# Output projections and side scores of the last layer, held back eight tiles instead of three and none

## The chip, the cores and the metric

The kernel runs on 1 core of one Trainium2 chip. The metric is the device time of one execution in microseconds (us). The time given is the median of three runs; the profile is of one further execution.

## The reference

Four layers follow each other, x = x + attention(layernorm(x)), over a sequence of 2048 rows of width 640 with 32 heads of 20 columns. Layers 0 and 2 attend in a causal window of 256 keys, layers 1 and 3 to all 2048 keys. The change is in layer 3, which computes:

```
def _B_ref(x, wqkv, wo):
    qkv = (x @ wqkv).reshape(B, S, 3, H, Dh).transpose(2, 0, 3, 1, 4)
    q, k, v = qkv[0], qkv[1], qkv[2]
    p = softmax(einsum("bhqd,bhkd->bhqk", q, k) * Dh ** -0.5)
    o = einsum("bhqk,bhkd->bhqd", p, v)
    return o.transpose(0, 2, 1, 3).reshape(B, S, D) @ wo
...
x = x + _B_ref(_layernorm(x), B_wqkv, B_wo)
```

## The kernel before

**Units and tiles.** The queries are cut into 4 chunks of 512 rows (c = 0 to 3), the heads into 8 groups of four (g = 0 to 7). A unit is one (layer, chunk, group). Its scores are made in banks: one block of 128 keys against 512 queries for one head fills one PSUM bank. A full unit has 16 key blocks x 4 heads = 64 banks. The main loop advances in tiles of three banks (rarely two or four): TensorE (PE) makes the scores of a tile (L1316), ScalarE (ACT) takes their exponential (L1347), and PE multiplies the exponentials of some tiles ago with the values (L1380). Tiles alternate between PSUM banks 0 to 2 and 3 to 5. Bank 7 collects a unit's output; bank 6 is left in the late stage for everything else.

**Side scores.** In layer 3, for c > 0 but for unit (3, 1, 0), six of the 64 banks of a unit (four in the very last unit) do not go through ACT. The generator `t_side` makes their scores one bank at a time in bank 6 (L912) and lets VectorE (DVE) compute the exponential by arithmetic (L918 to L946). It takes the units in order and works ahead of the main loop as far as the unit's keys and queries are loaded and one of five result buffers is free. Before, it waits only until the unit's loads have been issued (`loaded`) and the late stage has begun. At a unit's last bank, `side_need` forces whatever side scores are missing, and `side_done` forces their exponentials before the unit's last value products (L1389).

**Loads.** `load_ahead` issues the loads of the next unit (values L778, queries L790, keys L792, on SP's queue) when one of three buffers is free, which is when an earlier unit's last scores and values products have been issued.

**Normalise, pack, project.** When a unit ends, `finish_unit` casts its output from bank 7 into the tile `on` (L864). After every second unit `push_tail` starts `t_tail` for the pair: sums of the exponentials, reciprocal, spreading and scaling (L1090), in steps with waits of two tiles between them. Last comes `settle`: for the chunks 1 to 3 of layer 3, the scaled rows of four heads, which stand 32 partitions apart, are packed to dense rows of 128 by small transfers inside SBUF (L1103, SP's queue, nine for a pair). For the last two groups of chunk 3 nothing is packed. After the group that completes a chunk (g = 7), and after group 5 of chunk 3, `settle` waits three tiles (L1108) and then pushes the next task: `t_out`, the output projection of the chunk (matmuls by L300, added to x at L568, stored to HBM at L574), or `t_before_last`, the partial projection of the first six groups of chunk 3 (L591, L599). `t_out` makes eight pieces of 128 rows x 320 columns; with dense rows a piece is five row blocks of four matmuls.

**What sets the order.** All instructions are put out by one program, tile by tile, and each engine takes its own in that order. `state["tick"]` counts tiles. After each tile's exponential, `pump` runs tasks: first the tails that are awake, then the tasks of `todo` by due time, as far as a credit (0.45 a tile in this stage) reaches. `("wait", n)` puts a task to sleep until the tick has advanced by n. A task that uses bank 6 takes it by `take_m` and gives it back by `drop_m`. `keep_clock` fills tiles in which PE has little to do with matmuls that nobody reads (L300 masks,ident). Loops that force work (`require`, `side_need`, `side_done`) advance the tick without a tile when nothing is awake. `next_tile` makes a tile of four banks only when no tail exists and all tasks sleep.

Of the kernel before, what the change touches and what calls it, by code (L numbers as in the profile page):

```python
# [48 lines left out]
def kernel(  # L49
# [78 lines left out]
    def packed(l, c):  # L128

        return l == 3 and c > 0  # L130
# [56 lines left out]
    state = {"tick": 0, "held": None, "credit": 0.0, "early": True, "act": True, "unit": 0, "heat": 0.0, "carry": 0.0, "least": 0.0, "floor": 0.0, "owed": 0}  # L187
# [16 lines left out]
    def push(name, gen, need, left):  # L204
        lead = 0
        if type(name) is tuple and need <= first_use(1, NC - 1, 0):

            chain = {"out": True, "ln": name[1] == 1, "v": name[1] == 1 and name[-1] == 0}
            lead = 5 * chain.get(name[0], False)
            if name[0] in ("k", "q"):  # L210
                lead = 7 if name[1] == 1 and name[-1] == 0 else 2

            if name[0] == "stats" or name[:2] == ("ln", 0):
                lead = 5
        insort(todo, Task(name, gen, need, left, lead))
# [68 lines left out]
    def require(what):  # L284
        n = 0
        while what not in ready:
            n += 1
            assert n < 100000, what
            t = choose(False, state["unit"] if n < 400 else 1 << 30)
            if t is None:  # L290
                state["tick"] += 1
                continue
            state["credit"] = max(state["credit"] - advance(t), -1.0)
# [465 lines left out]
    def load_unit(u):  # L759

        l, c, g = u.l, u.c, u.g
        key = (l, c, g)
        if u.windowed:
            live["qa"] += 1
            live["ka"] += 1
            ka[c, g], qa[c, g] = ka_free.popleft(), qa_free.popleft()
            for j in range(4):
                rows = slice((4 * g + j) * DH, (4 * g + j + 1) * DH)
                strip = slice(32 * j, 32 * j + DH)
                nc.sync.dma_start(out=qa[c, g][strip, :], in_=q_d[l][c, rows, :])  # L770
                nc.sync.dma_start(
                    out=ka[c, g][strip, :], in_=k_d[l][rows, c * C : (c + 1) * C]
                )
            return
        k0, k1 = key_blocks(l, u.part)
        live["vt"] += 1
        vt[key] = kvp.tile([P, NT * 4 * VW], BF16, name="vt", tag="vt")
        nc.sync.dma_start(  # L778
            out=vt[key][:, k0 * 4 * VW : k1 * 4 * VW],
            in_=v_d[l][:, g, k0 * 4 * VW : k1 * 4 * VW],  # L780
        )
        live["kt"] += 1
        live["qt"] += 1
        kt[key] = kts[loads[0] % 3]
        qt[key] = qts[loads[0] % 4]
        loads[0] += 1
        for j in range(4):
            rows = slice((4 * g + j) * DH, (4 * g + j + 1) * DH)
            strip = slice(32 * j, 32 * j + DH)
            nc.sync.dma_start(out=qt[key][strip, :], in_=q_d[l][c, rows, :])  # L790
            cols = slice(k0 * P, k1 * P)
            nc.sync.dma_start(out=kt[key][strip, cols], in_=k_d[l][rows, cols])  # L792

    def unit_needs(u):
        l, c, g = u.l, u.c, u.g
        if (l, c) == (0, 0):
            return [("qk", l, c, g)]
        k0, k1 = key_blocks(l, u.part)
        chunks = range(k0 // 4, k1 // 4)
        blocks = range(80 * g // P, (80 * g + 79) // P + 1)  # L800
        if u.windowed:
            return [(n, l, c, b) for b in blocks for n in "qk"]
        return ["kts"] + [("q", l, c, b) for b in blocks] + [
            n
            for cc in chunks
            for n in [("k", l, cc, b) for b in blocks] + [("v", l, cc, g // 4)]
        ]

    loaded = set()

    def ensure_loaded(u, force):
        if id(u) in loaded:
            return
        needs = unit_needs(u)
        if force:
            for n in needs:
                require(n)
        elif any(n not in ready for n in needs) or any(
            live[t] >= cap[t] for t in (("ka", "qa") if u.windowed else ("kt", "vt", "qt"))
        ):  # L820
            return
        load_unit(u)
        loaded.add(id(u))

    def start_unit(u):
        for n in unit_needs(u):
# [47 lines left out]
    side = {"credit": 0.0, "gen": None, "tiles": None, "late": False}  # L874
# [22 lines left out]
    def t_side():  # L897

        V = nc.vector
        while aside:  # L900
            u = aside[0]
            for pair in range(len(u.aside) // 2):
                while id(u) not in loaded or (u.l == 3 and not side["late"]):
                    yield None
                for i in range(2):
                    yield "bank"
                    xi, xm, xw = side["tiles"]
                    if u.l == 3:
                        mseq[0] += 1
                        mfree[6] = (state["tick"] + 2, mseq[0])  # L910
                        kc, j = u.aside[2 * pair + i]
                        nc.tensor.matmul(  # L912
                            ps[:, 6, :], lhsT=u.k(kc, j), rhs=u.q(j, 0, 4), start=True, stop=True
                        )
                        side["psum"] = ps[:, 6, :]
                    scored = side.setdefault("scored", {})
                    scored[id(u)] = scored.get(id(u), 0) + 1
                    V.tensor_scalar(  # L918
                        out=xi.bitcast(I32)[:, i * C : (i + 1) * C], in0=side["psum"],
                        scalar1=SCALE * LOG2E * FIX, scalar2=-127.0 * FIX, op0=ALU.mult, op1=ALU.max,  # L920
                    )
                    yield 0.7
                V.tensor_scalar(
                    out=xm, in0=xi.bitcast(U16)[:, 0::2],
                    scalar1=E1 / FIX, scalar2=E0, op0=ALU.mult, op1=ALU.add,
                )
                yield 0.7
                power = xw.bitcast(I16)[:, 0 : 2 * C]
                V.tensor_scalar(
                    out=power, in0=xi.bitcast(I16)[:, 1::2],  # L930
                    scalar1=127.0, scalar2=128.0, op0=ALU.add, op1=ALU.mult,
                )
                yield 0.7
                V.scalar_tensor_tensor(
                    out=xi, in0=xm, scalar=EA, in1=xm, op0=ALU.add, op1=ALU.mult
                )
                yield 1.2
                while not side["out"]:
                    yield None
                pt = side["out"].popleft()  # L940
                po = pt.rearrange("p a b -> p (a b)")
                V.scalar_tensor_tensor(
                    out=po, in0=xi, scalar=EB, in1=xm, op0=ALU.add, op1=ALU.mult
                )
                yield 1.2
                V.tensor_tensor(out=po, in0=po, in1=power.bitcast(BF16), op=ALU.mult)  # L946
                side_out.setdefault(id(u), []).append(pt)
                yield 0.7
            aside.popleft()
# [145 lines left out]
    def settle(l, c, g, oT):  # L1095
        on = ons[l, c]
        if packed(l, c) and not ((l, c) == (3, NC - 1) and g >= G - 2):
            for j in range(4):
                r, a = (4 * g + j) * DH, 0
                while a < DH:  # L1100
                    b, o = divmod(r + a, P)
                    n = min(DH - a, P - o)
                    nc.sync.dma_start(  # L1103
                        out=on[o : o + n, b, :], in_=oT[32 * j + a : 32 * j + a + n, :]
                    )
                    a += n
            if g == G - 1 or (l, c, g) == (3, NC - 1, G - 3):
                yield ("wait", 3)  # L1108
        ready.add(("tail", l, c, g))
        if (l, c, g) == (3, NC - 1, G - 3):  # L1110
            push("before_last", t_before_last(), 0, 8.0)
        if g == G - 1:
            while any(("tail", l, c, n) not in ready for n in range(G)):
                yield ("wait", 1)
            need = first_use(l + 1, c, 0) if l < 3 else len(units) + c
            push(("out", l, c), t_out(l, c), need, 9.0)
            if l < 3:
                push_layer(l + 1, c)
# [82 lines left out]
    with tc.manual_schedule():  # L1201
# [17 lines left out]
        while n < last_layer:  # L1219
            size = 2 if len(tiles) % 2 and narrow(banks[n][0]) else 3  # L1220
            u = banks[n][0]
# [57 lines left out]
        while ended is None or t < ended + 8:  # L1279
# [3 lines left out]
            if t < len(tiles) or banks:  # L1283
# [9 lines left out]
                for b in cur:  # L1293
                    u = b[0]
# [69 lines left out]
            for n in range(2 if n_b == 0 or t > closed + 1 else 0):  # L1364
                u = pts[0][3][0] if pts else None
# [111 lines left out]
```

## Time and profile before

| | us |
|---|---|
| median of three runs (2224.45 to 2225.8) | 2225.43 |
| the profiled execution | 2229.77 |
| its span, first to last instruction | 2228.1 |
| busy: PE, DVE, ACT, POOL | 1933.2, 1200.5, 2141.2, 484.0 |
| mean granted clock of TensorE | 0.989 of full speed |

The last layer takes about the last 650 us of the span. In the profile's lines a group of instructions is given by its line, its engine, the operation and the tiles that it writes and reads; PEld is PE's loading of weights, SPq the queue on which SP issues transfers. "idle before" is the time in which the engine had nothing to do ahead of an instruction, with what released it. L300 is the line of a helper: the output projections, the sums and the fillers of the clock all carry it, and are told apart by their tiles (wop,on; sel,on; masks,ident).

### The profile page before, as it was taken

Reading aid. Unit: us, or ns where it says so; the run is one execution under the profiler, and the core shown is the slowest. Engines: PE = TensorE matmul, PEld = TensorE weight load, DVE = VectorE, ACT = ScalarE, POOL = GpSimd, SP = SyncE. Lnnn points to the kernel's source line nnn. Section 1 sums busy time; section 2 is a strip of 40 time slices with the busy share of each in tenths; the row PEclk is TensorE's granted clock in tenths of the full one; section 3 lists DMA queues with packets and bytes.
Section 4 is the critical chain, followed back from the end, with each engine's and each line's share of the span. In section 5 each row is a group of like instructions: output and inputs, shape, how many; then the busy total and the mean of one; then the engine's idle time right before and its main releaser. Section 6 shows DMA issues by size and latency. Waiting matters only on the chain.

```text
span 2228.1 us, 70079 instructions
## 1 busy us (share of the span) xinstructions
PE 1933.2 (87%) x30410; PEld 757.7 (34%) x30411; DVE 1200.5 (54%) x2190; ACT 2141.2 (96%) x1734; POOL 484.0 (22%) x950
## 2 busy tenths in 40 slices
PE   8889998988888888888888888888888888888888
PEld 4444443333333333333333433333322222222222
DVE  6656564434445455444554533532577767776774
ACT  7899899999999999999999999999999999999998
POOL 6664545200230114301143113511000000000000
PEclk9999999999999999999999999999999999999999
DMA  6233223321211223112230123122211111111100
GB/s 199 74 99 90 83 83 94 99 78 46 76 39 35 67 60 99 34 39 65 63 99 23 52 71 103 28 67 57 60 55 32 31 35 40 32 31 38 44 25 16
DMA packets 88404, 137.09 MB, mean 62 GB/s; under 512 B 20766, under 2 KB 63486, under 8 KB 88094
## 3 DMA queue, kind: packets, MB, share of 16 engines
q1 hardware_dynamic: 68878, 79.43, 12.8%
q0 software_dynamic: 19216, 53.17, 8.1%
q8 instruction: 238, 3.90, 0.7%
q14 instruction: 72, 0.59, 0.1%
HBM read 99.52 MB, written 27.79 MB: 57 GB/s over the span
## 4 chain that ended last, share of the span: by engine, by line
ACT 51%; PE 22%; issue 17%; DVE 7%; DMA 1%; POOL 1%; SPq 0%; ACTq 0%; DVEq 0%; POOLq 0%
ACT pt L1347 50%; PE ps L300 13%; PE ps L1316 6%; PE ps L1380 2%; DVE on L1090 1%; DVE st L323 1%; DVE pt L1429 1%; DMA wqk<-in_B_wqkv_dram 1%; PE ps L1086 1%; PE ps L437 0%; DVE x_sb L568 0%; DVE on L864 0%; SPq L1103 0%; DVE raw_o L918 0%; DVE xnT L323 0%
## 5 line engine op out<-in xcount | busy, mean ns | idle before, releaser
L1347 ACT ACTIVATE pt<-ps 128x1536 bf16<-128x1536 f32 (+2 forms) x1656 | 2104.2, 1456 | 55.4 <-PE ps L1316 45.7
L1316 PE MATMUL ps<-qt,kt 32*128 32x512 bf16 x3960 | 547.3, 386 | 91.1 <-ACT pt L1347 82.0
L300 PE MATMUL ps<-masks,ident 128*32 128x512 bf16 x5840 | 513.8, 389 | 118.3 <-ACT pt L1347 68.4
L1380 PE MATMUL ps<-pt,vt 128*21 128x512 bf16 x3904 | 400.0, 385 | 1.5 <-issue 1.0
L1316 PEld LDWEIGHTS <-kt 32*128 32x128 bf16 x3960 | 163.4, 91 | 551.4 <-issue 536.0
L300 PEld LDWEIGHTS <-ident 128*32 128x32 bf16 x5840 | 165.3, 94 | 351.8 <-issue 339.7
L1419 POOL TENSOR_SCALAR_AFFINE_SELECT pt<-pt 128x256 bf16<-128x256 bf16 (+2 forms) x505 | 214.8, 447 | 189.7 <-ACT pt L1347 187.0
L300 PE MATMUL ps<-xnT,wqk 128*32 128x512 bf16 x3320 | 225.3, 384 | 15.2 <-DVE st L323 4.0
L323 DVE CAST st<-ps 128x512 bf16<-128x512 f32 x134 | 92.7, 692 | 234.8 <-PE ps L300 228.3
L300 PE MATMUL ps<-wop,on 128*32 128x320 bf16 x3712 | 161.6, 303 | 11.9 <-DMA on<-on 5.0
L918 DVE TENSOR_SCALAR xnT<-ps 128x512 int32<-128x512 f32 x136 | 93.5, 688 | 134.2 <-PE ps L912 123.3
L1429 DVE TENSOR_TENSOR pt<-pt,masks 128x512 bf16<-128x512 bf16 (+4 forms) x267 | 112.9, 438 | 96.7 <-ACT pt L1347 94.5
L1380 PEld LDWEIGHTS <-vt 128*21 128x21 bf16 x3912 | 105.1, 91 | 125.0 <-issue 92.9
L568 DVE TENSOR_TENSOR x_sb<-x_sb,ps 128x320 bf16<-128x320 bf16 x120 | 58.3, 486 | 155.5 <-PE ps L300 155.2
L300 PEld LDWEIGHTS <-on 128*32 128x32 bf16 x5760 | 113.7, 95 | 80.9 <-issue 57.7
L1316 PE MATMUL ps<-qa,ka 32*128 32x384 bf16 (+2 forms) x1408 | 114.9, 275 | 27.5 <-ACT pt L1347 24.5
L300 PE MATMUL ps<-wv,xnT 128*32 128x320 bf16 x2560 | 115.2, 301 | 8.3 <-DVE on L1090 2.2
L1090 DVE TENSOR_TENSOR on<-on,ps 128x512 bf16<-128x512 bf16 x128 | 86.3, 683 | 58.3 <-PE ps L1086 56.1
L300 PEld LDWEIGHTS <-wqk 128*32 128x32 bf16 x3320 | 77.3, 96 | 114.6 <-issue 62.4
L864 DVE CAST on<-ps 128x512 bf16<-128x512 f32 x112 | 76.9, 687 | 66.2 <-PE ps L1389 41.9
L536 POOL DMA_DIRECT2D k_d<-st x75 | 43.0, 574 | 236.8 <-DVE st L323 226.9
L404 POOL TENSOR_SCALAR rstd<-mv 128x4 f32<-128x4 f32 x15 | 3.7, 249 | 381.6 <-DVE mv L391 373.4
(100 smaller groups left out, 1544.1 us busy)
## 6 DMA issues: line engine op xcount, KB each, us to landing
vt<-v_d SPq DMA_DIRECT2D x48, 336.0 KB
kt<-k_d SPq DMA_DIRECT2D x192, 80.0 KB
wqk<-in_B_wqkv_dram POOLq DMA_DIRECT2D x80, 160.0 KB, 3.4
wqk<-in_A_wqkv_dram POOLq DMA_DIRECT2D x70, 160.0 KB, 3.5
k_d<-st POOLq DMA_DIRECT2D x75, 128.0 KB, 2.6
q_d<-st POOLq DMA_DIRECT2D x75, 128.0 KB, 2.2
qt<-q_d SPq DMA_DIRECT2D x384, 20.0 KB
v_d<-vs POOLq DMA_DIRECT2D x16, 336.0 KB, 3.2
```

Of the source, the lines that this page charges most:

```text
L300: nc.tensor.matmul(out_[r], lhsT=lhsT[:, r], rhs=rhs, start=start, stop=stop)
L323: nc.vector.tensor_copy(out=out_, in_=in_)
L536: nc.gpsimd.dma_start(out=dst, in_=staging.pop())
L568: nc.vector.tensor_tensor(out=xv, in0=had, in1=yp, op=ALU.add)
L864: nc.vector.tensor_copy(out=oT, in_=op)
L918: V.tensor_scalar(out=xi.bitcast(I32)[:, i * C : (i + 1) * C], in0=side["psum"], scalar1=SCALE * LOG2E * FIX, scalar2=-127.0 * FIX, op0=AL ...
L1090: nc.vector.tensor_tensor(out=oT, in0=oT, in1=zb, op=ALU.mult)
L1316: nc.tensor.matmul(sp[:, i, col * P : (col + qn) * P], lhsT=u.k(kc, j), rhs=u.q(j, q0, qn), start=True, stop=True,)
L1347: nc.scalar.activation(out=pt[:, i:k, b0 * P :], in_=sp[:, i:k, b0 * P :], func=ACT.Exp, scale=SCALE,)
L1380: nc.tensor.matmul(op[32 * j : 32 * j + VW, q0 * P : (q0 + qn) * P], lhsT=u.v(kc, j), rhs=pg[:, i, col * P : (col + qn) * P], start=(first ...
L1419: nc.gpsimd.affine_select(out=v, in_=v, compare_op=ALU.is_gt if later else ALU.is_ge, fill=0.0, base=0, pattern=[[0, k - i], [-1 if later ...
L1429: nc.vector.tensor_tensor(out=pt_[:, i:k, cols], in0=pt_[:, i:k, cols], in1=mv_, op=ALU.mult)
```

## The change

The wait between packing and projecting grows from three tiles to eight. `loaded`, a set before, keeps the tick at which a unit's loads were issued, and the side scores of a unit of layer 3 start only eight ticks after it.

```diff
-    loaded = set()
+    loaded = {}
...
         load_unit(u)
-        loaded.add(id(u))
+        loaded[id(u)] = state["tick"]
...
             for pair in range(len(u.aside) // 2):
-                while id(u) not in loaded or (u.l == 3 and not side["late"]):
+                while id(u) not in loaded or (
+                    u.l == 3 and (not side["late"] or state["tick"] < loaded[id(u)] + 8)
+                ):
                     yield None
...
             if g == G - 1 or (l, c, g) == (3, NC - 1, G - 3):
-                yield ("wait", 3)
+                yield ("wait", 8)
         ready.add(("tail", l, c, g))
```

## The prediction

> **What bounds the kernel now.** I read the page's busy times first, then its costliest groups, then the view of waits after 1500 us (the last layer), and then the timeline and the stage table at the two places that the waits led to.
>
> ```profile
> PE 1933.2 (87%) x30410; PEld 757.7 (34%) x30411; DVE 1200.5 (54%) x2190; ACT 2141.2 (96%) x1734; POOL 484.0 (22%) x950
> ...
> L1347 ACT ACTIVATE pt<-ps 128x1536 bf16<-128x1536 f32 (+2 forms) x1656 | 2104.2, 1456 | 55.4 <-PE ps L1316 45.7
> ...
> L300 PE MATMUL ps<-wop,on 128*32 128x320 bf16 x3712 | 161.6, 303 | 11.9 <-DMA on<-on 5.0
> ```
>
> ACT is busy 96% of the span, with the exponentials of L1347. So an edit shortens the kernel only where it takes away ACT's idle time. The third line names the one operation that the change addresses: output projections that waited 5.0 us for the packing transfers. The waits after 1500 us, first PE's and then all of ACT's:
>
> ```profile
> PE ps L300 <- DMA on<-on: 5.0, 2, 2.5
> ...
> ACT pt L1347 <- PE ps L1316: 11.3, 13, 3.0
> ```
>
> The 5.0 us are two waits of 2.5 us. ACT lacks 11.3 us in the whole of the last layer, so that is nearly all there is to win. Asked by stretch, 5.4 of it lies between 1800 and 1900 us and 5.6 between 2000 and 2100, where the two waits are. The timeline at the first (start, length; idle before in brackets):
>
> ```profile
> 1819.72 6.83 SPq L1103 DMA_DIRECT2D on<-on  x9
> ...
> 1824.62 0.73 PE L300 MATMUL ps<-wop,on 128*32 128x320 bf16 x16
> 1827.87 0.32 PE L300 MATMUL ps<-wop,on 128*32 128x320 bf16 x4 [2.52 <-DMA on<-on]
> ```
>
> ```profile
> 1812.82 13.57 ACT L1347 ACTIVATE pt<-ps 128x1536 bf16<-128x1536 f32 x10
> 1828.83 2.82 ACT L1347 ACTIVATE pt<-ps 128x1536 bf16<-128x1536 f32 x2 [2.44 <-PE ps L1316]
> 1832.50 2.96 ACT L1347 ACTIVATE pt<-ps 128x1536 bf16<-128x1536 f32 x2 [0.85 <-PE ps L1316]
> 1835.93 2.96 ACT L1347 ACTIVATE pt<-ps 128x1536 bf16<-128x1536 f32 x2 [0.47 <-PE ps L1316]
> 1839.87 11.15 ACT L1347 ACTIVATE pt<-ps 128x1536 bf16<-128x1536 f32 x8 [0.97 <-PE ps L1316]
> ```
>
> SP is still issuing the nine packing transfers, 0.71 us apart, when PE starts the projection. Sixteen matmuls (four row blocks) pass, and the fifth block waits for the last transfer. PE takes its matmuls in order, so the next tile's scores stand behind it and ACT runs dry for 2.44 us. Then come three more gaps, with no transfer in sight. The stage table shows why (stretch, busy time of PE, PEld, DVE, ACT and POOL, then granted clock, DMA share, GB/s):
>
> ```profile
> 1825.00:1828.00 3.00, 0.48 (x16) 0.16 (x12) 0.32 (x1) 1.39 (x2) 0.00 (x0) 1.00 0.11 24
> ...
> 1830.00:1832.00 2.00, 1.79 (x15) 0.23 (x11) 1.54 (x3) 1.65 (x2) 0.00 (x0) 0.50 0.23 82
> ...
> 1838.00:1840.00 2.00, 2.00 (x27) 0.62 (x23) 1.15 (x2) 1.03 (x2) 0.00 (x0) 0.52 0.00 0
> 1840.00:1842.00 2.00, 1.94 (x36) 0.57 (x28) 1.76 (x4) 2.00 (x2) 0.00 (x0) 1.00 0.00 0
> ```
>
> Just after the wait the granted clock halves for some 10 us; PE is then full and late for every tile. The second place (2.52 us from 2039.3) has the same pair, 0.50 from about 2041.3 to 2051.5. In 1575 to 1825, 1856 to 2038 and 2070 to 2228 us the table gives 1.00.
>
> **The price of one stall.** Before the first place ACT did ten tiles in 13.57 us, 1.357 each. Its stream stops at 1812.82 + 13.57 = 1826.39 and is whole again at 1839.87. In these 13.48 us it did 6 tiles, worth 8.14, so 5.34 us are lost: 2.44 to the wait, 2.90 to the slow clock. At the second place ACT stops at 2040.37 and is whole at 2052.19 after 5 tiles. At the 6.84 / 5 = 1.368 us of the row before they are worth 6.84 of 11.82, so 4.98 us are lost: 3.02 to the wait, 1.96 to the clock. Together 10.3 us: 5.5 wait, 4.9 clock.
>
> **The longer wait, part by part.** It adds and removes no instruction and no DMA; it starts the projections of chunks 1 and 2, and the partial one of chunk 3, five tiles later. Five tiles are 5 x 1.357 = 6.8 us. The first projection then starts at 1824.6 + 6.8 = 1831.4 and its fifth block about 0.6 later, at 1832.0; the data were there at 1827.87. The margin is 4.1 us; at the second place 2038.6 + 6.8 + 0.6 = 2046.0 against 2041.85, again 4.1. Both stalls go, and with them, I take it, the clock drops: -10.3 us.
>
> What is late next: each pass is eight projections of 20 matmuls (0.86 us each), about 30 us long, so a later start moves its second half further past the end of a unit and into the next pair's normalisation, with which it shares PSUM bank 6 and DVE. Before already shows such meetings: 0.45 us of ACT idle at 1851.47, 0.94 at 2066.97 (the next projection waited 1.62 us for L568, behind L942 of 1.22 and L946 of 0.68), 0.4 near 1600. The bounds of what the shift does to these: at best all 1.8 us go too; at worst each of the two passes gets two more like the dearest, 4 x 0.94 = 3.8 us. I take +0.5, near the rows that exist, because the number of meetings hardly changes; only their place does.
>
> Chunk 3's partial projection (L591) waits only 0.2 us for its data. Moved by 6.8 us, it runs from 2198 to 2207.7 + 6.8 = 2214.5 at most. The last unit's output is cast at 2217.94, so it still ends before the final chain needs it; 3.4 us remain. Cover gone, each of its eight parts left over costs 0.72 us of PE. The one four-bank tile there (2.11 us at 2211.97) needs idle queues and may become three-bank tiles: 4 banks in the 1.76 us to the next tile against 4/3 x 1.357 = 1.81, so nothing.
>
> Meanwhile the tail stays in the queue five tiles longer. Nothing queues behind it: tails come once in two units (52 us from the packing issues at 1767.51 to those at 1819.72). On PE the five tiles are filled with the fillers of the clock (L300 masks,ident), as all tiles without a projection are. SP is not moved past anything: the transfers are issued where they were, and only the four output stores of each pass come later.
>
> **The side scores' wait.** No side score (L912) waits for a load in the trace; PE's waits there are on DVE alone (2.0 and 0.9 us). So nothing is to be gained. What it can delay: the first side score stands at 1578.16, its unit's loads at 1568.88 to 1572.7, six or seven tiles before, so it moves by one or two tiles. Its unit's sixth score (1597.19) is needed only when that unit ends, near 1631, so 34 us cover it. The other units' loads are far ahead: those of the last unit go out at 2141.68, its four side scores follow from 2168.30 on, 26 us or some 19 tiles later; the second unit's are loaded at 1577.14 and scored from 1603.38. I take 0; the ends are -0.9 and +0.9, the size of one meeting on DVE.
>
> **Sum.** -10.3 + 0.5 + 0 = -9.8 us. The profiled execution took 2229.77 us (span 2228.1, 1.7 around it), so it would come to about 2220.0. The median of the shown runs is 2225.43, 4.3 lower; the same -9.8 gives 2215.6 us, -0.44%.
>
> **A rule that speaks against half of this.** The row first: a PE gap of 2.52 us is followed by clock 0.50 twice. The Trainium skill, TensorE: Matmul & The Clock Gate, section "HAM oscillation — how this bites in real kernels", gives as the abstract rule that PE gaps should stay under about 3.4 us. By it a 2.5 us gap is harmless, the drop has another cause and stays, and the sum is -5.5 + 0.5: 2220.4. By the rows the drop belongs to the gap; I go with the rows, since the clock is whole elsewhere in this layer.
>
> **The rivals.**
> 1. The clock drops anyway (its cause is the load mix of the projection pass, not the gap). For it: near 898, 1168 and 1277 us the table shows drops too, where PE only missed 0.85 us here and 1.5 there. Against it: the pass near 1600 has 1.00 throughout. Then only the waits go: 2225.4 - 5.5 + 0.5 = 2220.4. Chance 0.10.
> 2. The later pass collides with the next pair's normalisation and the side scores hard enough to halve the clock by itself, as near 1168 after gaps of 0.85 and 0.43 us. Each place pays 2 to 3 us of clock and two meetings of 0.94: 2 x (2.5 + 1.9) = 8.8 given back, 2215.1 + 8.8 = 2223.9. Against it: the second half of the pass already runs there at 1.00. Chance 0.11.
> 3. The wait doesn't do what it says: it counts the scheduler's ticks, and forced loops advance ticks without a tile. From the first issue to the last landing it takes 1827.87 - 1819.72 = 8.15 us, six tiles; if fewer than two of the five added ticks are real tiles, a shorter stall stays. Then 2224 to 2225.5. For it: only that such loops exist. Chance 0.05.
> 4. Slower: the held-back side scores come due at a unit's end. There the scheduler forces what is missing, and PE and ACT wait for DVE: one pair is 2 x 0.69 + 0.69 + 0.69 + 1.22 + 1.22 + 0.68 = 5.9 us. It decides from two such forced pairs on (11.8 against 9.8); from three on it shows, 17.7 - 9.8 = +7.9, 2233.3. Against it: the load leads of 19 tiles and more, and 34 us of slack at the first unit. Chance 0.05.
>
> **How the numbers follow.** The forecast holds 0.69, and lies by itself between 2213 (the meetings gone too, -1.8) and 2219 (3.8 of them new). For 8 in 10, rival 1 goes in, and the nearer half of rival 2: 2212.8 to 2222.5. About 0.2% (4.45 us) is what a measurement of this kernel tells from no change, so faster means under 2221.0: the forecast with 0.68, rival 1 with 0.08, rival 2 with 0.01, in all 0.77. Within 0.2%: rivals 1 (0.02), 2 (0.10) and 3 (0.05) and 0.01 of the forecast, 0.18. Slower by 0.2%: rival 4 alone, 0.05.
>
> **What would show it.** Right: no "DMA on<-on" among PE's waits; ACT idle after 1500 us down from 11.3 to about 1 to 3 us; granted clock 1.00 from 1575 us on; first projection matmuls of chunks 1 and 2 about 12 us after the first packing issue instead of 4.9 (1819.72 to 1824.62); the last L591 before the last L864. Wrong: clock 0.50 near 1835 or 2045 without a DMA wait (rival 1 or 2); ACT gaps at unit ends with PE behind L942 or L946 (rival 4); an L591 after the last unit.

## The result, and the profile after

The changed kernel takes 2215.88 us (median of 17 runs, 2210.82 to 2227.0) against 2228.07 us (17 runs, 2223.6 to 2235.04) for the kernel before on the same chips. The ratio is 0.9948 with a 95% interval of 0.9937 to 0.996, so between 8.9 and 14.0 us of 2228 are gone. Forecast were 9.8.

The page of the changed kernel (lines moved by two from L923 on, so L1347 is now L1349):

```profile
PE 1919.8 (87%) x30415; PEld 756.1 (34%) x30415; DVE 1199.8 (54%) x2190; ACT 2139.9 (97%) x1734; POOL 482.5 (22%) x950
...
L1349 ACT ACTIVATE pt<-ps 128x1536 bf16<-128x1536 f32 (+2 forms) x1657 | 2104.3, 1456 | 41.8 <-PE ps L1318 32.1
...
L300 PE MATMUL ps<-wop,on 128*32 128x320 bf16 x3712 | 159.8, 301 | 7.1 <-DVE x_sb L568 4.0
```

ACT does the same work (2139.9 us, 2141.2 before) in a shorter span; its idle time ahead of the exponentials went from 55.4 to 41.8 us. The projections no longer wait for "DMA on<-on"; what they wait for most is now their own earlier pieces on DVE, 4.0 us in the whole execution (3.3 before). The first place, in the timeline of the changed kernel:

```profile
1814.41 6.82 SPq L1105 DMA_DIRECT2D on<-on  x9
...
1827.04 0.86 PE L300 MATMUL ps<-wop,on 128*32 128x320 bf16 x20
...
1828.50 0.86 PE L300 MATMUL ps<-wop,on 128*32 128x320 bf16 x20
```

The first piece starts 12.6 us after the first packing issue instead of 4.9 and runs through all its twenty matmuls. ACT's timeline there and at the second place:

```profile
1798.92 40.88 ACT L1349 ACTIVATE pt<-ps 128x1536 bf16<-128x1536 f32 x30
...
2004.48 46.21 ACT L1349 ACTIVATE pt<-ps 128x1536 bf16<-128x1536 f32 x34
2051.63 49.91 ACT L1349 ACTIVATE pt<-ps 128x1536 bf16<-128x1536 f32 x37 [0.94 <-PE ps L1318]
```

Thirty and 34 exponentials in a row, where before the row broke after every one or two. The gap of 0.94 us at the second place was there before too. All of ACT's waits in the last layer, then the stage table at the first place (busy times, then granted clock):

```profile
ACT pt L1349 <- PE ps L1318: 2.4, 6, 0.9
```

```profile
1826.00:1830.00 4.00, 3.67 (x65) 1.66 (x65) 3.96 (x7) 4.00 (x4) 0.00 (x0) 1.00 0.00 0
1830.00:1845.00 15.00, 12.94 (x193) 4.03 (x192) 11.89 (x18) 14.47 (x12) 0.00 (x0) 1.00 0.24 74
```

**A yardstick that leaves the rest out.** The two profiled executions differ by 15.4 us of span, more than the medians, because the clock also dropped at other places in the layers before, and differently in each execution. Both kernels issue the same instructions up to the one four-bank exponential that writes ka near 1570 us. It stands, before and after, here:

```profile
1575.33 2.21 ACT L1347 ACTIVATE ka<-ps 128x2048 bf16<-128x2048 f32 x1
```

```profile
1569.81 2.21 ACT L1349 ACTIVATE ka<-ps 128x2048 bf16<-128x2048 f32 x1
```

So 5.5 us of the difference were there before the change could act. From this point to the end of the span it is 2228.1 - 1575.33 = 652.8 us before and 2212.7 - 1569.81 = 642.9 after: 9.9 us less. The experiments are compared by this stretch.

### The profile page after: what moved, and what is told of

Same layout as the page of the kernel before. It is cut to its first block, busy times and chain, and to the rows that moved or that the text cites. A ratio compares the mean times of both kernels' runs of the same rounds, so it can differ in the third digit from the quotient of the medians.

```text
span 2212.7 us, 70085 instructions
## 1 busy us (share of the span) xinstructions
PE 1919.8 (87%) x30415; PEld 756.1 (34%) x30415; DVE 1199.8 (54%) x2190; ACT 2139.9 (97%) x1734; POOL 482.5 (22%) x950
## 4 chain that ended last, share of the span: by engine, by line
ACT 52%; PE 21%; issue 18%; DVE 6%; DMA 1%; POOL 1%; ACTq 0%; DVEq 0%; POOLq 0%
ACT pt L1349 51%; PE ps L300 12%; PE ps L1318 5%; PE ps L1382 2%; DVE on L1092 1%; DVE st L323 1%; DVE pt L1431 1%; DMA wqk<-in_B_wqkv_dram 1%; PE ps L1088 1%; PE ps L437 0%; DVE on L864 0%; DVE x_sb L568 0%; DVE raw_o L920 0%; POOL pt L1421 0%; DVE xnT L323 0%
## 5 line engine op out<-in xcount | busy, mean ns | idle before, releaser
L1349 ACT ACTIVATE pt<-ps 128x1536 bf16<-128x1536 f32 (+2 forms) x1657 | 2104.3, 1456 | 41.8 <-PE ps L1318 32.1
L568 DVE TENSOR_TENSOR x_sb<-x_sb,ps 128x320 bf16<-128x320 bf16 x120 | 58.3, 486 | 146.8 <-PE ps L300 146.6
L536 POOL DMA_DIRECT2D k_d<-st x75 | 43.0, 573 | 233.2 <-DVE st L323 223.2
```

What stands on the lines that cost most here:

```text
L536: nc.gpsimd.dma_start(out=dst, in_=staging.pop())
L568: nc.vector.tensor_tensor(out=xv, in0=had, in1=yp, op=ALU.add)
L1349: nc.scalar.activation(out=pt[:, i:k, b0 * P :], in_=sp[:, i:k, b0 * P :], func=ACT.Exp, scale=SCALE,)
```

## The experiments

| run | stretch, us | ACT idle in it | PE's wait on on<-on | half clock at the two places | ratio to before (95%) |
|---|---|---|---|---|---|
| before | 652.8 | 11.3 | 5.0 | both, 10.2 and 10.2 us | |
| after | 642.9 | 2.4 | none | none | 0.9948 (0.9937-0.996) |
| after, again | 642.0 | 1.6 | none | none | 0.996 (0.9946-0.9973) |
| longer wait alone | 643.4 | 1.9 | none | none | 0.9957 (0.9946-0.9968) |
| side wait alone | 652.4 | 11.1 | 5.6 | both, 10.2 and 6.8 us | 1.0001 (0.9992-1.0011) |
| early, no rows of the last transfers | 641.9 | 1.9 | none | none | 0.9963 (0.9951-0.9976) |
| four tiles | 649.2 | 8.8 | 5.2 | second only, 6.8 us | 1.0001 (0.9988-1.0015) |
| six tiles | 647.8 | 7.4 | 4.9 | first only, 6.8 us | 0.9986 (0.9972-1.0) |
| 24 tiles | 646.9 | 1.1 | none | none | 0.9977 (0.9965-0.9989) |
| side wait of 48 | 775.1 | 130.0 | none | many | one run, 2350.2 us |
| packing on POOL's queue | 645.7 | 4.5 | none | none | 0.994 (0.9919-0.9961) |
| gap filled | 649.8 | 9.3 | 1.7 | none | 0.9983 (0.9974-0.9992) |
| 24 tiles, chunk 3 eight | 641.2 | 0.7 | none | none | 0.9949 (0.9937-0.9961) |

In the early run and in the one on POOL's queue the partial projection of chunk 3 still waits 0.2 to 0.6 us for its transfers, as before; the column leaves that out. The column on the clock counts the drops right behind the two waits; single drops of 3.4 us elsewhere are named below.

**The two parts apart.** Longer wait alone, in the kernel before:

```diff
-                yield ("wait", 3)
+                yield ("wait", 8)
```

> The longer wait alone; the side scores start as before. The yardstick is the stretch from the four-bank tile (the one exponential that writes ka near 1570 us, which both kernels issue at the same place and ahead of anything changed) to the end of the span: 652.8 us before (2228.1 - 1575.33), 642.9 after (2212.7 - 1569.81). My theory (the whole gain is the longer wait): 642 to 644 us, no wait on on<-on, ACT idle after 1500 us between 1 and 3 us, clock 1.00 at both passes. Rival (the side scores' wait brings part of it): 645 us or more.

Measured: 643.4 us and ratio 0.9957. The other part alone, in the changed kernel:

```diff
-                yield ("wait", 8)
+                yield ("wait", 3)
```

> The side scores' wait alone, with three tiles before the projections. My theory: as before, 651 to 654 us from the four-bank tile to the end, two waits of about 2.5 us on on<-on and two clock drops. Rival (the side scores' wait brings part of it): 650 us or less.

Measured: 652.4 us and ratio 1.0001, with waits of 2.9 and 2.7 us on the transfers. So the longer wait is the whole gain, and the side scores' wait neither gains nor costs anything that these runs can tell (its interval is 0.9992 to 1.0011). The changed kernel run once more beside others:

> The changed kernel as it is, beside the other two on the same chip: 642 to 644.5 us from the four-bank tile to the end, and a ratio to the kernel before between 0.993 and 0.996.

It gave 642.0 us and 0.996, both as expected.

**Is it the gap?** The pass left where it was, without its need of the last rows:

```diff
-                        yp, on[:, g, qb * P : (qb + 1) * P],
+                        yp, on[:, min(g, 2) if dense else g, qb * P : (qb + 1) * P],
```

> The kernel before, with the wait of three tiles, but the dense projections read the third row block again in place of the fourth and fifth, so they need no row of the last transfers (that part of the output projection of chunks 1 and 2 is computed from other rows). The pass stands exactly where it stood. My theory (the missing rows are the whole cause, the clock drop included): no wait on on<-on, clock 1.00 from the four-bank tile on, 642 to 644 us from there to the end. Rival (the clock drops because of what the pass does and where it stands, not because of the gap): the two drops stay, 646 to 648 us.

It leaves out the fourth and fifth row blocks, so only its time is of use. Measured: 641.9 us, and the stage table has the clock whole at both places (the first here):

```profile
1822.00:1826.00 4.00, 3.78 (x65) 1.47 (x64) 3.71 (x6) 4.00 (x5) 0.00 (x0) 1.00 0.09 21
1826.00:1836.00 10.00, 8.76 (x132) 3.07 (x124) 8.37 (x13) 10.00 (x9) 0.00 (x0) 1.00 0.08 24
```

The pass begins where it began before, 249.3 us after the four-bank tile, and an early pass is as good as a late one if it finds its rows. The place of the pass does not lower the clock; the wait for the rows does. Next, the wait kept but PE given something to do ahead of it:

```diff
+                for _ in range(11 if dense and qb + i == 0 else 0):
+                    by_columns(ps[:, mb, :], ident, masks[:, 0, :], True, True)
                 yp = ps[:, mb, 0:HD]
```

> The kernel before, wait of three tiles, side scores as before; ahead of the first projection of chunks 1 and 2 PE gets eleven groups of filler matmuls that nobody reads (about 0.22 us each, 2.4 us), so it works while the last transfers land and does not stand still. ACT is held up as before. My theory (the clock halves because PE stands still, so a filled gap costs its length alone): wait on on<-on under 0.5 us, clock 1.00 at both passes, ACT idle of 2 to 2.6 us at each, 646.5 to 648.5 us from the four-bank tile to the end. Rival (the clock follows from the delay itself or from the pass): a drop at one or both, 649 us or more.

Measured: 649.8 us, 1.3 more than expected. The stage table of that run around the first place:

```profile
1819.00:1826.00 7.00, 6.57 (x116) 2.78 (x116) 3.86 (x6) 4.40 (x4) 0.00 (x0) 1.00 0.09 21
1826.00:1830.00 4.00, 3.44 (x47) 0.85 (x35) 2.80 (x5) 3.97 (x4) 0.00 (x0) 1.00 0.12 41
```

ACT loses 2.60 us there and 3.68 at the second place, where 1.4 us of wait were left behind the fillers:

```profile
1825.49 19.29 ACT L1349 ACTIVATE pt<-ps 128x1536 bf16<-128x1536 f32 x14 [2.60 <-PE ps L1318]
...
2037.82 20.56 ACT L1349 ACTIVATE pt<-ps 128x1536 bf16<-128x1536 f32 x15 [3.68 <-PE ps L1318]
2059.94 1.45 ACT L1349 ACTIVATE pt<-ps 128x1536 bf16<-128x1536 f32 x1 [1.55 <-PE ps L1318]
```

Yet the clock stays whole behind both. What is over the expectation is a drop of 3.4 us at 2058, on the last pieces of the second pass and at the end of a unit. It follows a wait of PE of 1.62 us for L568 and made the 0.94 us gap there 1.55 + 0.44. So an ACT stall of about the old length without PE standing still costs its length: it is PE's rest that lowers the clock. Two places alone could be luck, since two of eight waits elsewhere were followed by no drop either. But in the ten timed runs the mean granted clock was 0.994, against 0.991 for the kernel before and 0.993 for the changed kernel beside it. The timed ratio, 0.9983, lies between before and after, as it should.

**How long must the wait be?** First four tiles:

```diff
-                yield ("wait", 3)
+                yield ("wait", 4)
```

> Four tiles in place of three, side scores as before. The gap of 2.52 us should shrink by one tile of 1.36 to about 1.2 us at each of the two places. My theory (a long gap halves the clock, and gaps of 1.6 us were seen without a drop): two waits of about 1.2 us, no drop of the clock there, 644.5 to 646.5 us from the four-bank tile to the end, so two thirds or more of the gain from one tile. Rival (any gap on the transfers halves the clock): drops stay and 649 us or more.

That missed. The gap did not shrink at all, and the clock dropped at one place of two. PE's timeline at both places:

```profile
1823.17 0.73 PE L300 MATMUL ps<-wop,on 128*32 128x320 bf16 x16
1826.42 0.32 PE L300 MATMUL ps<-wop,on 128*32 128x320 bf16 x4 [2.53 <-DMA on<-on]
...
2037.71 0.46 PE L300 MATMUL ps<-wop,on 128*32 128x320 bf16 x4 [2.71 <-DMA on<-on]
```

The first packing issue stands at 1818.29, so the pass began 4.88 us after it, as with three tiles (4.90). A new theory was tried with six tiles (the same line with 6):

> Six tiles in place of three, side scores as before. The run with four tiles left the pass where it was: its first matmuls still came 4.9 us after the first packing issue. My theory now (the pass can only take PSUM bank 6 where the side scores leave it free, one slot in six tiles, so waits of three to six tiles all start it in the same slot and eight reach the next one): first projection 4.9 us after the first packing issue again, two waits of 2.5 to 2.9 us, 647 to 654 us from the four-bank tile to the end, depending on whether the clock drops. Rival (each tile of wait moves the pass by a tile; the run with four was an accident): first projection some 9 us after the first issue, no or a very short wait, 642 to 645 us.

```profile
1817.71 0.45 PE L300 MATMUL ps<-wop,on 128*32 128x320 bf16 x8
...
1821.87 0.46 PE L300 MATMUL ps<-wop,on 128*32 128x320 bf16 x4 [2.78 <-DMA on<-on]
```

The pass began 3.98 us after the first issue (1813.73), the waits were 2.78 and 2.10 us, and the stretch 647.8. Counted from the four-bank tile (1568.42 here), the first projection stands at 249.29 us with three, four and six tiles alike, and at 257.23 with eight. With six the packing came 0.9 us later, hence 3.98 where 4.9 had been expected. So the pass moves by slots and not by tiles of wait: that is shown. What makes the slots is read with the code and was not tested by itself: while side scores run, a pair of them reserves bank 6 at ticks two apart, and only one slot in six tiles is left for a projection. The times fit it: the pass starts two tiles after the second score of a pair, 249.29 after 246.3 us and 257.23 after 254.5. With three to six tiles the pass starts in one slot, with eight in the next; 24 tiles are the other end.

> Twenty-four tiles in place of three, side scores as before. My theory: no wait on the transfers at chunks 1 and 2, but the partial projection of chunk 3 (L591) now falls behind the last unit's scores, and its eight pieces of 0.72 us are paid at the end: 646 to 650 us from the four-bank tile to the end, the last L591 after the last unit's cast. Rival (a longer wait costs nothing): 642 to 644 us.

Measured: 646.9 us with ACT nearly unbroken (1.1 us idle). The loss is behind the last unit, in PE's timeline:

```profile
2202.02 0.60 PE L1391 MATMUL ps<-ka,vt 128*21 128x512 bf16 x4
...
2206.07 2.36 PE L300 MATMUL ps<-wop,on 128*32 128x320 bf16 x64
```

```profile
2205.19 0.60 PE L1389 MATMUL ps<-ka,vt 128*21 128x512 bf16 x4
2205.72 0.72 PE L591 MATMUL ps<-wop,on 128*128 128x320 bf16 x4
...
2212.12 2.90 PE L591 MATMUL ps<-wop,on 128*128 128x320 bf16 x20
2214.95 2.36 PE L300 MATMUL ps<-wop,on 128*32 128x320 bf16 x64
```

The first fence is the changed kernel, with 4.05 us between the last unit's last values and the last projection. The second is the run with 24 tiles, with 9.76, and all eight pieces of L591 in between: 5.7 us, the eight times 0.72 of the prediction. Hence the mixed version:

```diff
-                yield ("wait", 8)
+                yield ("wait", 24 if c < NC - 1 else 8)
```

> The changed kernel with 24 tiles for chunks 1 and 2 and 8 for chunk 3. The run with 24 everywhere lost 16.4 us from ACT's last exponential to the end where the changed kernel lost 10.7, and had only 1.1 us of ACT idle before it. My theory (the two add up): 640.5 to 642.5 us from the four-bank tile to the end, about 1 us less than the changed kernel, which the timed runs will hardly tell apart. Rival (the later pass pays elsewhere): 643 us or more.

Measured: 641.2 us with 0.7 us of ACT idle left, the shortest stretch of all and inside the expected range. That it is better than eight tiles everywhere is not shown: three profiles with eight tiles spread from 642.0 to 643.4, and its ratio, 0.9949, cannot be told from the changed kernel's 0.996 beside it.

**The side scores' wait, driven until it hurts**, with 48 in place of 8 in the changed kernel:

```diff
-                    u.l == 3 and (not side["late"] or state["tick"] < loaded[id(u)] + 8)
+                    u.l == 3 and (not side["late"] or state["tick"] < loaded[id(u)] + 48)
```

> The changed kernel with 48 ticks in place of 8 between a unit's loads and its side scores. Unit ends come some 19.5 tiles apart and loads two to three units ahead, so the scores become due within the last tiles of their unit and are forced there. My theory (the fourth rival of the prediction is real, and only the long lead of the loads kept it away): ACT idles at nearly every unit's end behind PE and DVE, 1 to 6 us at each of some 20 units: 665 to 760 us from the four-bank tile to the end. Rival (forced work fills itself in): under 655 us.

```profile
ACT pt L1349 <- PE ps L1318: 126.9, 53, 14.5
```

Measured: 775.1 us, 15 over the upper end. The largest stall is 14.5 us, at the first unit; those at the other units' ends are mostly 2 to 8 us long, and the clock drops behind most of them. The slower rival was a real mechanism; at a wait of eight ticks the lead of the loads kept it away. Where between 8 and 48 it begins was not measured.

**Another way to the same gain.** Wait of three tiles, packing from POOL:

```diff
-                    nc.sync.dma_start(
+                    nc.gpsimd.dma_start(
                         out=on[o : o + n, b, :], in_=oT[32 * j + a : 32 * j + a + n, :]
```

> The kernel before, wait of three tiles, side scores as before; only the packing transfers are issued on POOL's queue, which does nothing in this layer, instead of SP's, where nine loads of 0.37 us stand ahead of them (1816.26 to 1819.6). The scaling that they need (L1090) ends at 1815.3, so the first can go out 4 us earlier and the last data land near 1824, a little ahead of the fifth row block at 1825.3. My theory (the gap is the loads' time on SP's queue; it goes without any longer wait): wait on on<-on under 1 us, clock 1.00 at both passes, 642 to 645 us from the four-bank tile to the end. Rival (the transfers themselves are too slow for a wait of three tiles on any queue): waits of 1.5 us and more, 647 us and more.

```profile
1816.66 2.52 POOL L1103 DMA_DIRECT2D on<-on  x5 [42.08 <-DVE on L1090]
1823.70 2.00 POOL L1103 DMA_DIRECT2D on<-on  x4 [4.52 <-DVE on L1090]
```

The last issue ends at 1825.70, which is 242.3 us after this run's four-bank tile (1583.42); before it was 1826.55 - 1575.33 = 251.2. So the transfers go out 8.9 us earlier and the projections at 1832.71 find their rows. The expectation named nine loads on SP's queue; in fact SP stood still even earlier, on a load that waited for its buffer, and the first five transfers waited behind that. The stretch, 645.7, is 0.7 over the expected range. The clock stays whole where the waits had been, but two drops of 3.4 us at unit ends (1881.9, and 2066.2 on the last pieces of the second pass) go with an ACT idle of 4.5 us, where the three runs with eight tiles have 1.6 to 2.4. The timed ratio, 0.994, is the changed kernel's.

## Why the prediction was right, and where it was not

**What bounds the kernel: right.** ACT's busy time did not change, and its idle time in the last layer fell from 11.3 to 2.4 us (1.9 and 1.6 in the two further runs with eight tiles).

**The price of the stall: right in sum, its halves measured roughly.** 10.3 us were forecast for two stalls, 5.5 wait and 4.9 clock. The stretch fell by 9.4 to 10.8 us in the three runs with eight tiles. With the gap filled the wait alone was paid: ACT idle 2.60 + 3.68 and no drop behind it. Its stretch of 649.8, less about 1.05 for the drop at 2058 (1.55 + 0.44 in place of 0.94), is 648.7. By this estimate the clock was worth 4.1 us (652.8 less 648.7) and the wait 5.3 to 6.7, from one profile each. In the profiles with a gap one drop or two remained, and the stretch read 647.8 (one), 649.2 (one), 652.4 and 652.8 (two), so a half is not known to better than some 2 us.

**The median: close by luck.** The forecast of 2215.6 us and the measured 2215.88 agree by luck. The 9.8 us were taken from 2225.43, the median of three runs; 17 runs of the kernel before gave 2228.07, and the saving measured is 8.9 to 14.0 us.

**Five tiles and a margin of 4.1 us: the size was wrong.** The step "Five tiles are 5 x 1.357 = 6.8 us" took each tile of wait for a tile of delay. Measured are 7.7 us (12.63 against 4.90 after the first issue) at the first place, because the start snaps to slots. For eight tiles this only added margin; for four to six, by the same reckoning, the forecast would have been wrong outright, as the run with four showed.

**What is late next, +0.5: right in kind, small in size.** The meetings at unit ends stayed: 0.46 at 1840.26 and 0.94 at 2051.63, the latter with the same 1.62 us of PE waiting for L568. In the two further runs with eight tiles ACT's idle is within 0.2 us of the 1.8 counted before. In the profiled run there is one more thing, a clock drop of 3.4 us at 1877, which came with 0.7 us of idle and did not come in the two other runs with eight tiles. One reading there was wrong: a pass is not "about 30 us long" at both places. In the kernel before its first and last projections start 48.8 us apart at the first place (1824.62 to 1873.43) and 28.5 at the second; in the changed kernel 44.6 and 39.5.

**Chunk 3: right.** The last L591 starts at 2197.39, the last unit's cast at 2202.66. The four-bank tile there became three-bank tiles; no cost of it can be seen in the stretch.

**The side scores' wait: right at 0.** It moved the first side score by three to four tiles (7.7 us after the four-bank tile instead of 2.8), a little more than the one or two forecast, under 34 us of cover.

**The rivals.** Rival 1, that the clock drops whatever the gap, is refuted by the early run without the gap and by the filled gap. Rival 2, that the later pass halves the clock by itself, shows in small: single drops of 3.4 us at unit ends in some executions (1877 after, 1882 and 2066 with POOL, 2058 with the gap filled), worth some 1 to 3 us a run, not 8.8. Two of them (2058 and 2066) follow the wait of 1.62 us for L568, which stands in ten of the profiles and has no drop behind it in the other eight. Rival 3 did not hold for eight tiles but was nearer the truth than I allowed: the wait does not count what it seems to, for another reason than the one named. Rival 4 did not show at 8 ticks and did at 48.

**The rule against it.** The Trainium skill (TensorE: Matmul & The Clock Gate, "HAM oscillation — how this bites in real kernels") would have let a gap of 2.5 us pass. Here gaps of 2.10 to 2.86 us were followed by half clock at six places of eight, so the rows decide: the rule's 3.4 us is not a safe limit for a gap in this kernel.

## What to carry to other kernels

A stall of TensorE in a stage that fills ACT has two prices, the wait itself and the slow clock after it, and the second can be as large as the first (2.90 beside 2.44 us at the first place); read the granted clock for 10 us behind every gap of PE. The remedy need not be a later consumer: an earlier producer (another queue) or work that PE can do in the gap takes away all or a part of it. A wait counted in ticks moves work only as far as the next free slot of what that work needs, so look for the resource that it competes for before trusting the count.

## What the runs showed of the hardware

**A drop goes with how little of PE's array worked in one stretch of 3.4 us.** The clock changes in the records stand 3.41 us apart or a multiple of it, so a gap falls into these stretches in one way or another. The kernel before at its two places, then the run with four tiles at its first and second place, each the stretch of 3.4 us up to where a drop could come (busy time of PE first):

```profile
1826.30:1829.70 3.40, 1.79 (x34) 0.92 (x35) 1.47 (x2) 0.96 (x2) 0.00 (x0) 1.00 0.05 12
2037.90:2041.30 3.40, 1.43 (x27) 0.43 (x19) 1.37 (x2) 2.47 (x2) 0.00 (x0) 1.00 0.13 30
```

```profile
1824.90:1828.30 3.40, 1.83 (x34) 0.92 (x35) 1.51 (x2) 0.95 (x2) 0.00 (x0) 1.00 0.05 12
...
2033.10:2036.50 3.40, 1.60 (x27) 0.55 (x26) 1.84 (x3) 2.94 (x3) 0.00 (x0) 1.00 0.13 30
```

And two stretches of the changed kernel, the first followed by a drop, the second not:

```profile
1873.80:1877.20 3.40, 2.27 (x31) 0.72 (x26) 1.78 (x3) 3.40 (x4) 0.00 (x0) 1.00 0.30 103
...
2047.90:2051.30 3.40, 1.78 (x38) 0.81 (x30) 2.54 (x4) 2.79 (x2) 0.00 (x0) 1.00 0.58 177
```

PE was busy 1.79, 1.43, 1.60 and 2.27 us of 3.40 ahead of drops, and 1.83 and 1.78 where none came, so its busy time does not settle it. How much of the array the matmuls fill does sort these six. Count each matmul by its columns times the share of 128 x 128 that its form takes: one of 128*32 128x320 counts 320 / 4 = 80. Then the stretches ahead of drops come to about 2730, 2470, 2690 and 2620, the two others to 2820 and 2960.

The same count was taken for every stretch at full clock between 130 and 2195 us in the twelve profiles other than that with 48 ticks, 7158 in all. All 42 under 2490 were followed by half clock, 22 of the 50 between 2490 and 2840, and none above. (In the run with 48 ticks 19 drops stand behind counts under 2620, and one stretch of 2340 had none.) The median in the last layer is about 3600, so a rest of 2.5 us inside one stretch can be enough here. This is a fit to the records, in which the ends of matmuls are modelled; no run varied this count alone.

**Most of the spread goes with the clock.** Over the 17 runs of the changed kernel the time falls as the mean granted clock rises: 2227.0 us at 0.989, 2215.88 at 0.994, 2210.82 at 0.998 (correlation -0.94). A difference of 1 us between kernels is not to be had from such times. The stretch between two fixed instructions leaves the layers before out, but it too spread by 1.4 us in three profiles with eight tiles.

**A DMA queue is held up by its head.** SP issues in order, so packing transfers that were ready (their scaling had ended at 1808.3 for the first group of the pair) waited for a load whose buffer came free at 1816. On POOL's queue the first five went out 233.2 us after the four-bank tile, on SP's 244.4. POOL issued the same transfers in 0.51 us each against SP's 0.71.
